# Reordering VectorE, TensorE and GpSimd work where an attention kernel hands over to its first expert

## The chip, the cores and the metric

One Trainium2 chip (trn2), one core. The metric is the device time of one execution in microseconds. Times before are the median of three runs; the profile is one more execution of the same program, taken by the hardware profiler.

## The reference

Eight batches of eight heads of 576 tokens go through masked attention; the result, seen as 4608 rows of 512, is routed to one of eight experts each (top 1), and the expert's two-layer network is scaled by two gates.

```python
scores = np.where(masks, scale * q @ k.T, -1e9)
attn = exp(scores - max) / (sum + 1e-9)
x = (attn @ v).transpose(0, 2, 1, 3).reshape(4608, 512)
logits = x @ w_gate;  e_idx = argmax(logits, axis=1)
gate_w = softmax(logits)[arange, e_idx]
eom = sigmoid(x @ w_output_gate)
for e in range(8):
    mask = e_idx == e
    h = maximum(x[mask] @ w1[e], 0)          # 512 -> 1024
    out[mask] = gate_w * eom[:, e] * (h @ w2[e])   # 1024 -> 512
```

## The kernel before

**Attention and gating.** `attention()` walks 8 batches in 5 steps each. Behind each batch `gating()` computes the choice of expert for 576 tokens, laid out as 96 partitions by 6 columns. It gives each token a slot number among the tokens of its expert, makes one-hot tables of the slots (`hit`: 128 places and 48 pages), and multiplies them with values to be delivered (`named`, line 694). Matmuls on TensorE (`place`, line 593) add these up into `book`, a table of token numbers and gates by place, page and expert. The gate is a 32-bit number, so `parted()` (line 684) cuts it into three bf16 parts: copy, subtract, copy, subtract, copy; each part is one of the last three values of `book`. In the batches up to the second to last this runs beside attention. In the last batch (`last`) nothing of attention is left, and the order of the statements from line 741 on is the order in which each engine sees its work.

**The lead.** After four batches the expert with the most tokens (the lead) is known, and its first 256 rows can start early: `lead_layer()` (line 503) is a generator that issues its first layer in pieces between other work, in single-pass float32. Its eight blocks of 128 hidden columns are taken in four pairs; two pairs' sums live in two PSUM banks (tile `sp`). When a pair is done, `flush()` empties the bank: ScalarE writes the rounded positive part to `hha`, VectorE the difference to `hla`. The fourth pair reuses the second pair's bank, so TensorE must wait for the second pair's `hla`. `fill(n)` advances the generator by n matmuls, each of which is two records in the trace. With `hold[0]` set (from the last batch's second half on), flushes are put off; the list `LF` says how many matmuls are issued at which point of the last gating. The end of it reads, from line 748:

```python
for _ in weights(): pass     # 3 small VectorE operations: the gate
parted()                     # 5 on GpSimd
counts(); count_on()
hold[0] = False
for v in range(2, 2 + WP): name(v)    # 3 on VectorE
fill(LF[1])                  # 11 matmuls, flushes among them
count()
enter(place(2, 2 + WP), 2, 2 + WP)
```

**The experts.** `experts()` (line 1267) first gathers the lead's other rows by indirect DMAs on GpSimd's queue (`gather(0)`, line 158). Weights and activations are split in a high and a low float32r half (`split`, line 994: ScalarE casts, another engine subtracts), and each product is three matmuls: high by high, low by high, high by low. The first 256 rows of the lead go through the second layer as two blocks of 128 rows (`by_token`, `tokens_in`, lines 1109 and 1127), each 8 columns j by 3 matmuls into one PSUM bank. Within the second block the gathered rows are turned (`turn`), and the two last quarters of w1 are split; `TURN_AT` says behind which column. Then come the eight ranks r. For r = 0 the first layer of the lead's other rows runs as 8 columns of 12 matmuls (`layer1`, `products`), rotating over four PSUM banks `hps`. Behind column 3 `copied()` (line 985) makes copies of the page table by 12 matmuls into the bank `hps[3]`, which VectorE copies out; they are read at the second layer of the rank (`by_tail`, line 1156). From there on ranks follow each other, with the next rank's loads, splits and turns within the second layer of the one before.

Of the kernel before, what the change touches and what calls it, by code (L numbers as in the profile page):

```python
# [20 lines left out]
E = 8  # L21
# [5 lines left out]
QB = 96  # L27
# [7 lines left out]
EB = 4  # L35
HALVED = B
STEADY = B - 2
# [5 lines left out]
PN = 4  # L43
LF = (4, 11, 4, 3)
TURN_AT = (1, 3, 4, 6)
# [15 lines left out]
def attn_moe_kernel(  # L61
# [56 lines left out]

    NC = 2 * B - HALVED + 1
    cum = const.tile([QB + 2, NC, E], BF16, name="cum")  # L120
# [52 lines left out]
    def attention():  # L173
        with ExitStack() as actx:
# [234 lines left out]
            def logits(b, hf):  # L409
# [23 lines left out]
                yield 0  # L433
                if b < HALVED and hf == 1:
                    yield from gating(b, 0, NB, b)
                if b >= HALVED:
                    yield from gating(b, JH * hf, JH * (hf + 1), 2 * b - HALVED + hf)

            def count():
                cp = ps_g.tile([128, 512], F32, name="gp")  # L440
                nc.tensor.matmul(out=cp[:, 0:E], lhsT=tri[0:QB, 1, :], rhs=cum[0:QB, 2 * B - HALVED, :], start=True, stop=True)
                nc.vector.tensor_copy(out=cnt, in_=cp[:, 0:E])
# [60 lines left out]
            def lead_layer():  # L503
# [17 lines left out]
                for j in range(0, FC, 2):  # L521
# [14 lines left out]
                    done.append((slice(j, j + 2), hp, []))  # L536
                    if not hold[0]:
                        flush(j + 2)
# [3 lines left out]
            def gating(b, j0, j1, ci):  # L542
# [141 lines left out]
                def parted():  # L684
                    left = wall[:, tcols]
                    for i in range(WP):
                        P.tensor_copy(out=parts[:, i, :], in_=left)
                        if i + 1 < WP:
                            P.tensor_tensor(out=rest[:, i, :], in0=left, in1=parts[:, i, :], op=ALU.subtract)
                            left = rest[:, i, :]  # L690
# [36 lines left out]
                else:  # L727
# [6 lines left out]
                    if not last:  # L734
                        for _ in weights():
                            pass
                        parted()
                        for v in range(2, 2 + WP):
                            name(v)
                    else:  # L740
                        fill(LF[0])
                        wp = place(0, 2)
                        enter(before, 0, 2 + WP)
                        exp_sum()
                        enter(wp, 0, 2)
                        for _ in tokens_first(0, HB, idx0):
                            pass
                        for _ in weights():
                            pass
                        parted()  # L750
                        counts()
                        count_on()
                        hold[0] = False
                        for v in range(2, 2 + WP):
                            name(v)
                        fill(LF[1])
                        count()
                        enter(place(2, 2 + WP), 2, 2 + WP)
                if ci == EB - 1:
# [7 lines left out]
            def fill(n):  # L767
                for _ in range(n):
                    for g in fillers[:1]:
                        if next(g, 1):  # L770
                            fillers.clear()
# [221 lines left out]

    def split(hi, lo, src, eng=nc.vector):
        nc.scalar.copy(out=hi, in_=src)  # L995
        eng.tensor_tensor(out=lo, in0=src, in1=f32(hi), op=ALU.subtract)  # L996

# [42 lines left out]

    def split_w(r, which, c, eng=nc.vector):
        raw = raws[r, which, c]
        if which == 1:
            split(w1h[:, c, :], w1l[:, c, :], raw, eng)
        else:
            sl = slice(2 * c, 2 * c + 2)
            split(w2h[:, sl, :].rearrange("p c f -> p (c f)"), w2l[:, sl, :].rearrange("p c f -> p (c f)"), raw)
# [57 lines left out]
    def trio(i):  # L1105
        hh, hl = hs[i]
        return (hh, w2h), (hl, w2h), (hh, w2l)

    def tokens_in(yp, i, o, m, between={}):
        for j in range(FC):  # L1110
            for q, (h, w) in enumerate(trio(i)):
                nc.tensor.matmul(out=yp[0:m, :], lhsT=h[:, j, o:o + m], rhs=w[:, j, :],  # L1112
                                 start=(j == 0 and q == 0), stop=(j == FC - 1 and q == 2))
            for fn, *a in between.get(j, ()):
                fn(*a)
# [10 lines left out]

    def by_token(i, o, m, w, row, between={}):
        yp = rotate(yps)
        tokens_in(yp, i, o, m, between)
        return lambda: store(yp, w, row, m)  # L1130
# [136 lines left out]
    def experts():  # L1267
# [10 lines left out]
        for c in range(2):  # L1278
            split_w(0, 1, c)
        by_token(0, 0, 128, lead_gate[:, 0:1], tabe[:, 0:1])()  # L1280
        between = {j: [(turn, 0, c, m)] for j, (c, m) in zip(TURN_AT, blocks(0))}
        between[5] = [(arms, 0)]
        for c in range(2, KC):
            between[TURN_AT[c - 2]].append((split_w, 0, 1, c, nc.gpsimd))
        sent = [by_token(0, 128 * c, 128, lead_gate[:, c:c + 1], tabe[:, c:c + 1], between) for c in range(1, EH // 128)]
# [3 lines left out]
        for r in range(E):  # L1289
# [12 lines left out]
            for j in range(FC):  # L1302
                layer1(r, j)
                if r == 0 and j == 1:
                    count_spare()
                    send_away()
                if r == 0 and j == 3:
                    copied()
# [191 lines left out]
```

## Time and profile before

| | |
|---|---|
| median of 3 runs | 624.65 us (624.39 to 625.74) |
| the profiled execution, its own time | 624.76 us |
| span of its trace | 622.5 us |
| mean granted TensorE clock | 0.985 |
| TensorE (PE) busy | 580.3 us, 93% |
| VectorE (DVE) busy | 308.8 us, 50% |
| ScalarE (ACT) busy | 278.1 us, 45% |
| GpSimd (POOL) busy | 202.2 us, 32% |

The span runs from the first to the last instruction; 2.26 us of the execution's time lie outside it. Attention with its gatings takes the first 170 us, the hand-over to the first expert some 30 us, the ranks the rest, with the last matmuls near 609 us. A record of an instruction has its start, its duration, and in brackets the idle time of its engine just before it with what ended that.

### The profile page before, as it was taken

What the parts mean: (1) busy time and instruction counts of PE and PEld (TensorE: products, weight loads), DVE (VectorE), ACT (ScalarE), POOL (GpSimd) and SP (SyncE); (2) the same over time, 40 slices, a digit from 0 to 9 for tenths busy, and PEclk for the clock granted to TensorE, in tenths of its full rate; (3) what the DMA queues carried; (4) which work ended last, traced back from release to release, by engine and by line L of the source; (5) the groups of instructions that cost most, each with busy time, mean ns of one, the idle gap of its engine ahead of it and who ended that gap; (6) DMA issues with size and microseconds to landing.
All of it is one profiled execution on the core that took longest, in us unless ns stands there. A gap on an engine that the chain in (4) does not pass through costs nothing. (4 is left out here: it accounts for less than half of the span.)

```text
span 622.5 us, 14509 instructions
## 1 busy us (share of the span) xinstructions
PE 580.3 (93%) x5670; PEld 490.8 (79%) x5670; DVE 308.8 (50%) x699; ACT 278.1 (45%) x553; POOL 202.2 (32%) x282
## 2 busy tenths in 40 slices
PE   8898999899849999999999999999999999999990
PEld 6676776777538889988998899889988878888880
DVE  4888888987637553443143325334533542442500
ACT  3877877766225243433243224334243443443310
POOL 4327766665324424011401140225023124021030
PEclk9999999999979999999999999999999999999996
DMA  9989999893422846144305430553064164161010
GB/s 319 311 291 293 310 298 296 291 296 121 160 63 74 326 125 189 35 160 140 127 22 169 153 115 5 183 133 115 14 221 141 55 220 140 49 227 43 3 42 17
DMA packets 42488, 97.93 MB, mean 157 GB/s; under 512 B 5458, under 2 KB 16346, under 8 KB 42394
## 3 DMA queue, kind: packets, MB, share of 16 engines
q1 hardware_dynamic: 34122, 73.47, 36.3%
q0 software_dynamic: 6864, 19.74, 9.6%
q10 hardware_dynamic: 1408, 3.38, 1.5%
q8 instruction: 71, 1.16, 0.8%
q14 instruction: 23, 0.19, 0.1%
HBM read 77.74 MB, written 20.58 MB: 158 GB/s over the span
## 5 line engine op out<-in xcount | busy, mean ns | idle before, releaser
L1078 PE MATMUL hp<-xl,w1h 128*128 128x256 f32 (+8 forms) x384 | 126.9, 330 | 0.1
L1078 PE MATMUL hp<-xh,w1h 128*128 128x256 f32 (+8 forms) x384 | 127.0, 331 | 0.0
L1078 PE MATMUL hp<-xh,w1l 128*128 128x256 f32 (+8 forms) x384 | 126.9, 330 | 0.0
L1112 PE MATMUL yp<-w2h,hhb 128*128 128x512 f32 (+1 forms) x208 | 83.2, 400 | 0.0
L1112 PE MATMUL yp<-w2l,hhb 128*128 128x512 f32 (+1 forms) x208 | 81.3, 391 | 0.0
L1112 PE MATMUL yp<-w2h,hlb 128*128 128x512 f32 (+1 forms) x208 | 81.1, 390 | 0.0
L1199 POOL DMA_INDIRECT out_dram<-ys,idx x32 | 32.9, 1029 | 132.7 <-ACT ys L1198 128.2
L1199 POOL DMA_INDIRECT out_dram<-ys,ri x18 | 20.3, 1126 | 169.4 <-ACT ys L1198 166.3
L1078 PEld LDWEIGHTS hp<-xl,w1h 128*128 128x128 f32 x384 | 72.6, 189 | 3.4 <-DVE xl L996 0.4
L1078 PEld LDWEIGHTS hp<-xh,w1h 128*128 128x128 f32 x384 | 72.6, 189 | 3.4 <-ACT xh L995 0.3
L1078 PEld LDWEIGHTS hp<-xh,w1l 128*128 128x128 f32 x384 | 72.6, 189 | 2.8
L996 DVE TENSOR_TENSOR xl<-tp,xh 128x512 fp32r<-128x512 f32 (+3 forms) x40 | 25.8, 650 | 88.1 <-ACT xh L995 84.4
L995 ACT CAST xh<-tp 128x512 fp32r<-128x512 f32 (+3 forms) x40 | 22.0, 555 | 99.2 <-PE tp L1055 96.0
L1101 DVE SCALAR_TENSOR_TENSOR hlb<-hp,hhb 128x384 fp32r<-128x384 f32 (+3 forms) x48 | 28.2, 590 | 68.1 <-ACT hf L1100 64.2
L1098 ACT ACTIVATE hhb<-hp 128x384 fp32r<-128x384 f32 (+3 forms) x48 | 24.9, 518 | 81.8 <-PE hp L1078 73.5
L309 POOL TENSOR_TENSOR p_t<-p_t,st 128x512 f32<-128x512 f32 x40 | 42.6, 1064 | 52.0 <-DVE cum L584 15.2
L158 POOL DMA_INDIRECT xg<-xd,idx x40 | 44.0, 1101 | 23.9 <-DVE f L665 9.9
L1112 PEld LDWEIGHTS yp<-w2l,hhb 128*128 128x128 f32 (+1 forms) x208 | 38.8, 187 | 8.7
L1112 PEld LDWEIGHTS yp<-w2h,hhb 128*128 128x128 f32 (+1 forms) x208 | 38.9, 187 | 8.1 <-issue 0.4
L1198 ACT ACTIVATE ys<-yp,pages 128x512 f32<-128x512 f32 (+1 forms) x36 | 24.9, 692 | 45.0 <-issue 35.5
L1112 PEld LDWEIGHTS yp<-w2h,hlb 128*128 128x128 f32 (+1 forms) x208 | 38.9, 187 | 7.7
L996 DVE TENSOR_TENSOR w1l<-raw,w1h 128x1024 fp32r<-128x1024 f32 x30 | 36.7, 1225 | 11.7 <-ACT w1h L995 11.3
(213 smaller groups left out, 1079.0 us busy)
## 6 DMA issues: line engine op xcount, KB each, us to landing
raw<-in_moe_w_dram SPq DMA_DIRECT2D x54, 512.0 KB
vst<-in_vs_dram SPq DMA_DIRECT2D x8, 780.0 KB
vlt<-in_vl_dram SPq DMA_DIRECT2D x16, 292.5 KB
q_t<-in_ql_dram SPq DMA_DIRECT2D x8, 576.0 KB
q_t<-in_qs_dram SPq DMA_DIRECT2D x7, 650.0 KB
xd<-x_t SPq DMA_DIRECT2D x80, 54.0 KB
xd<-x_t SPq DMA_DIRECT2D x16, 256.0 KB
raw<-in_moe_w_dram ACTq DMA_DIRECT2D x6, 512.0 KB
```

Of the source, the lines that this page charges most:

```text
L158: nc.gpsimd.indirect_dma_start(out=dst, out_offset=None, in_=src, in_offset=bass.IndirectOffsetOnAxis(ap=idx, axis=0), bounds_check=top, o ...
L309: nc.gpsimd.tensor_tensor(out=p_t, in0=p_t, in1=st, op=ALU.subtract)
L995: nc.scalar.copy(out=hi, in_=src)
L996: eng.tensor_tensor(out=lo, in0=src, in1=f32(hi), op=ALU.subtract)
L1078: nc.tensor.matmul(out=hp[:, 0:n], lhsT=w[:, k, 128 * j:128 * (j + 1)], rhs=x[:, k, 0:n], start=first, stop=(k == KC - 1 and w is w1l))
L1098: nc.scalar.activation(out=hh[:, j, 0:s], in_=hp[:, 0:s], func=AF.Relu)
L1101: nc.vector.scalar_tensor_tensor(out=hl[:, j, 0:s], in0=hp[:, 0:s], scalar=0.0, in1=f32(hh[:, j, 0:s]), op0=ALU.max, op1=ALU.subtract)
L1112: nc.tensor.matmul(out=yp[0:m, :], lhsT=h[:, j, o:o + m], rhs=w[:, j, :], start=(j == 0 and q == 0), stop=(j == FC - 1 and q == 2))
L1198: nc.scalar.activation(out=ys[0:m, 0:n], in_=yp[0:m, 0:n], func=AF.Copy, scale=w[0:m, :])
L1199: i = nc.gpsimd.indirect_dma_start(out=out.rearrange("t (k d) -> (t k) d", k=k), out_offset=bass.IndirectOffsetOnAxis(ap=row, axis=0), in_ ...
```

## The change

It does four things. (1) In the last batch's gating, the lead's held flushes are allowed before the gate is computed (`hold[0] = False` and one of the matmuls come forward), the gate's parts are made on VectorE instead of GpSimd, behind the matmuls' flushes, and the count of tokens goes behind the last `place`. The flush of the fourth pair moves to the generator's end. (2) In the lead's first block of the second layer the matmuls with the low half of w2 stand two columns later (`lag=2`). (3) The last two quarters of the lead's w1 get their low half from VectorE instead of GpSimd. (4) The copies of the page table are made behind column 5 instead of 3. A constant (`HALVED`) that had no effect is gone.

```diff
-LF = (4, 11, 4, 3)
+LF = (4, 10, 4, 3)
...
                     done.append((slice(j, j + 2), hp, []))
-                    if not hold[0]:
+                    if not hold[0] and j + 2 < FC:
                         flush(j + 2)
                     yield
                 flush(FC)
...
                 def parted():
                     left = wall[:, tcols]
                     for i in range(WP):
-                        P.tensor_copy(out=parts[:, i, :], in_=left)
+                        W.tensor_copy(out=parts[:, i, :], in_=left)
                         if i + 1 < WP:
-                            P.tensor_tensor(out=rest[:, i, :], in0=left, in1=parts[:, i, :], op=ALU.subtract)
+                            W.tensor_tensor(out=rest[:, i, :], in0=left, in1=parts[:, i, :], op=ALU.subtract)
                             left = rest[:, i, :]
...
                         for _ in tokens_first(0, HB, idx0):
                             pass
+                        hold[0] = False
+                        fill(1)
                         for _ in weights():
                             pass
-                        parted()
                         counts()
                         count_on()
-                        hold[0] = False
+                        fill(LF[1])
+                        parted()
                         for v in range(2, 2 + WP):
                             name(v)
-                        fill(LF[1])
+                        enter(place(2, 2 + WP), 2, 2 + WP)
                         count()
-                        enter(place(2, 2 + WP), 2, 2 + WP)
...
-    def tokens_in(yp, i, o, m, between={}):
+    def tokens_in(yp, i, o, m, between={}, lag=0):
+        todo = [[] for _ in range(FC + lag)]
         for j in range(FC):
-            for q, (h, w) in enumerate(trio(i)):
-                nc.tensor.matmul(out=yp[0:m, :], lhsT=h[:, j, o:o + m], rhs=w[:, j, :],
-                                 start=(j == 0 and q == 0), stop=(j == FC - 1 and q == 2))
-            for fn, *a in between.get(j, ()):
+            for q, hw in enumerate(trio(i)):
+                todo[j + (lag if q == 2 else 0)].append((j, *hw))
+        order = [p for ps in todo for p in ps]
+        for n, (j, h, w) in enumerate(order):
+            nc.tensor.matmul(out=yp[0:m, :], lhsT=h[:, j, o:o + m], rhs=w[:, j, :],
+                             start=(n == 0), stop=(n == len(order) - 1))
+            for fn, *a in between.get(n // 3, ()) if n % 3 == 2 else ():
                 fn(*a)
...
-        by_token(0, 0, 128, lead_gate[:, 0:1], tabe[:, 0:1])()
+        by_token(0, 0, 128, lead_gate[:, 0:1], tabe[:, 0:1], lag=2)()
...
-            between[TURN_AT[c - 2]].append((split_w, 0, 1, c, nc.gpsimd))
+            between[TURN_AT[c - 2]].append((split_w, 0, 1, c))
...
-                if r == 0 and j == 3:
+                if r == 0 and j == 5:
                     copied()
```

`W` is VectorE in the last batch and GpSimd in all others, so only the last batch's parts move.

VectorE, end of the last gating (`idx` holds the row numbers for the gathers, `f` and `wall` the gate, `cum` the running counts). Before:

```order
L455 TENSOR_SCALAR idx_70<-tn 128x6
L663 TENSOR_SCALAR f<-f 96x6
L665 SCALAR_TENSOR_TENSOR f<-f 96x6
L668 RECIPROCAL wall<-f 96x6
L575 TENSOR_REDUCE s_3468<-oh 96x8
L584 TENSOR_TENSOR cum<-cum,s_3468 96x8
L694 TENSOR_TENSOR named<-hit,parts 96x6x48 x3
L513 SCALAR_TENSOR_TENSOR hla<-sp,hha 128x512 x3
L442 COPY cnt<-gp 128x8
L604 TENSOR_TENSOR book<-book,gp 128x144
L996 TENSOR_TENSOR w2l<-hhb,w2h 128x1024 x2
```

With the change, first from `idx` on:

```order
L452 TENSOR_SCALAR idx_70<-tn 128x6
L510 SCALAR_TENSOR_TENSOR hla<-sp,hha 128x512
L660 TENSOR_SCALAR f<-f 96x6
L662 SCALAR_TENSOR_TENSOR f<-f 96x6
L665 RECIPROCAL wall<-f 96x6
L572 TENSOR_REDUCE s_3468<-oh 96x8
```

and then from `cum` to the low half of w2:

```order
L581 TENSOR_TENSOR cum<-cum,s_3468 96x8
L510 SCALAR_TENSOR_TENSOR hla<-sp,hha 128x512
L684 CAST parts<-wall 96x6
L686 TENSOR_TENSOR rest<-wall,parts 96x6
L684 CAST parts<-rest 96x6
L686 TENSOR_TENSOR rest<-rest,parts 96x6
L684 CAST parts<-rest 96x6
L691 TENSOR_TENSOR named<-hit,parts 96x6x48 x3
L601 TENSOR_TENSOR book<-book,gp 128x144
L439 COPY cnt<-gp 128x8
L510 SCALAR_TENSOR_TENSOR hla<-sp,hha 128x512
L994 TENSOR_TENSOR w2l<-hhb,w2h 128x1024 x2
```

The three differences of the lead stood in a row behind the names; now the second pair's stands right behind `idx`, the third's ahead of the five operations on the parts, the fourth's behind `book` and `cnt`. TensorE's order around it keeps its 11 matmuls in a row; only the count's matmul moved behind the six of `place`.

TensorE, first matmuls of the lead's first block in the second layer, before:

```order
L1112 MATMUL yp_3614<-w2h,hha 128x512
L1112 MATMUL yp_3614<-w2h,hla 128x512
L1112 MATMUL yp_3614<-w2l,hha 128x512
L1112 MATMUL yp_3614<-w2h,hha 128x512
L1112 MATMUL yp_3614<-w2h,hla 128x512
```

and with the change:

```order
L1114 MATMUL yp_3614<-w2h,hha 128x512
L1114 MATMUL yp_3614<-w2h,hla 128x512
L1114 MATMUL yp_3614<-w2h,hha 128x512
L1114 MATMUL yp_3614<-w2h,hla 128x512
L1114 MATMUL yp_3614<-w2l,hha 128x512
```

The first matmul with the low half of w2 is the fifth instead of the third.

TensorE, the copies of the page table, before:

```order
L1078 MATMUL hp_3613<-xh_3605,w1l 128x408
L1256 UNCONDITIONAL_BRANCH
L991 MATMUL hp_3613<-pages,ident 64x96 x2
L991 MATMUL hp_3613<-pages,ident 32x96 x4
L1256 COMPARE_AND_BRANCH x2
L1078 MATMUL hp_3610<-xh_3605,w1h 128x480
```

and with the change:

```order
L1076 MATMUL hp_3611<-xh_3605,w1l 128x408
L1258 UNCONDITIONAL_BRANCH
L989 MATMUL hp_3613<-pages,ident 64x96 x2
L989 MATMUL hp_3613<-pages,ident 32x96 x4
L1258 COMPARE_AND_BRANCH x2
L1076 MATMUL hp_3612<-xh_3605,w1h 128x480
```

The bank written by the copies (`hp_3613`, `hps[3]`) was the one that the matmul just ahead had filled; now the matmul ahead fills another one (`hp_3611`).

## Rows read from the trace of the kernel before

**Rows 1.** The page: TensorE's busy time, share, instructions; and its waits from 210 us on.

```profile
PE 580.3 (93%) x5670; PEld 490.8 (79%) x5670; DVE 308.8 (50%) x699; ACT 278.1 (45%) x553; POOL 202.2 (32%) x282
...
PE tp L1055 <- PEq L1172: 0.6, 2, 0.3
```

**Rows 2.** Timeline of TensorE: start, duration, line, operation, [idle before, released by].

```profile
165.59 1.90 PE L528 MATMUL sp<-xe,raw 128*128 128x256 f32 x8
168.40 1.53 PE L528 MATMUL sp<-xe,raw 128*128 128x256 f32 x6
177.35 5.57 PE L528 MATMUL sp<-xe,raw 128*128 128x256 f32 x16 [7.43 <-DVE hla L513]
...
184.71 0.47 PE L1112 MATMUL yp<-w2h,hha 128*128 128x512 f32 x1 [1.39 <-DVE book L604]
...
185.81 0.50 PE L1112 MATMUL yp<-w2l,hha 128*128 128x512 f32 x1 [0.39 <-DVE w2l L996]
...
190.93 0.39 PE L1112 MATMUL yp<-w2h,hha 128*128 128x512 f32 x1
...
192.29 0.60 PE L1055 MATMUL tp<-ident,xg 128*128 128x128 f32 x4
```

**Rows 3.** Timeline of VectorE in the same stretch.

```profile
169.65 0.17 DVE L455 TENSOR_SCALAR idx<-tn 128x6 int32<-128x6 f32 x1
...
170.45 0.16 DVE L584 TENSOR_TENSOR cum<-cum,s 96x8 bf16<-96x8 bf16 x1
171.41 0.46 DVE L694 TENSOR_TENSOR named<-hit,parts 96x288 bf16<-96x288 bf16 x1 [0.79 <-POOL parts L687]
...
176.62 0.68 DVE L513 SCALAR_TENSOR_TENSOR hla<-sp,hha 128x512 fp32r<-128x512 f32 x1
...
184.27 0.30 DVE L604 TENSOR_TENSOR book<-book,gp 128x144 f32<-128x144 f32 x1
184.53 2.36 DVE L996 TENSOR_TENSOR w2l<-hhb,w2h 128x1024 fp32r<-128x1024 f32 x2
```

**Rows 4.** Timeline of GpSimd: the gathers of the lead's rows between the parts.

```profile
170.09 1.08 POOL L158 DMA_INDIRECT xg<-xd,idx  x1 [9.92 <-DVE f L665]
...
171.54 1.21 POOL L158 DMA_INDIRECT xg<-xd,idx  x1 [0.16 <-issue]
```

**Rows 5.** Timeline of ScalarE: the fourth pair's flush and the high half of w2.

```profile
182.96 0.60 ACT L512 ACTIVATE hha<-sp 128x512 fp32r<-128x512 f32 x1 [4.97 <-PE gp L441]
183.46 1.98 ACT L995 CAST w2h<-hhb 128x1024 fp32r<-128x1024 f32 x2
```

**Rows 6.** Stretches: length, busy PE, PEld, DVE, ACT, POOL, granted clock, DMA share, GB/s.

```profile
174.50:181.00 6.50, 3.65 (x9) 2.93 (x10) 2.11 (x4) 0.60 (x1) 1.58 (x3) 0.50 0.23 74
...
183.00:186.00 3.00, 1.22 (x9) 0.63 (x7) 2.41 (x5) 3.00 (x4) 0.00 (x0) 1.00 0.00 0
...
178.00:179.00 1.00, 1.00 (x4) 0.82 (x3) 0.69 (x1) 0.00 (x0) 0.00 (x0) 0.50 0.00 0
...
217.00:218.00 1.00, 1.00 (x7) 1.00 (x6) 0.54 (x1) 0.42 (x2) 0.00 (x0) 1.00 0.15 45
```

**Rows 7.** Timeline of TensorE in the lead's first layer and at its end.

```profile
207.16 0.35 PE L1078 MATMUL hp<-xl,w1h 128*128 128x408 f32 x1
207.35 0.35 PE L1078 MATMUL hp<-xh,w1l 128*128 128x408 f32 x1
209.16 0.69 PE L991 MATMUL hp<-pages,ident 128*64 128x96 f32 x12 [1.47 <-DVE hlb L1101]
209.78 0.45 PE L1078 MATMUL hp<-xh,w1h 128*128 128x408 f32 x1
...
220.74 1.09 PE L1055 MATMUL tp<-ident,xg 128*128 128x128 f32 x8
```

**Rows 8.** VectorE: waits from 186 to 200 us (total, times, longest); the last difference.

```profile
DVE xl L996 <- ACT xh L995: 3.2, 4, 1.1
...
198.12 0.56 DVE L996 TENSOR_TENSOR xl<-tp,xh 128x384 fp32r<-128x384 f32 x1 [0.62 <-ACT xh L995]
```

More of the change, by code (lines that the diff above doesn't have):

```diff
@@ L35 @@
 EB = 4
-HALVED = B
 STEADY = B - 2
@@ L117, in attn_moe_kernel @@
     wts, eidx = (ecst[:, i, :] for i in range(2))
-    NC = 2 * B - HALVED + 1
+    NC = B + 1
     cum = const.tile([QB + 2, NC, E], BF16, name="cum")
@@ L433, in logits @@
                 yield 0
-                if b < HALVED and hf == 1:
+                if hf == 1:
                     yield from gating(b, 0, NB, b)
-                if b >= HALVED:
-                    yield from gating(b, JH * hf, JH * (hf + 1), 2 * b - HALVED + hf)
             def count():
                 cp = ps_g.tile([128, 512], F32, name="gp")
-                nc.tensor.matmul(out=cp[:, 0:E], lhsT=tri[0:QB, 1, :], rhs=cum[0:QB, 2 * B - HALVED, :], start=True, stop=True)
+                nc.tensor.matmul(out=cp[:, 0:E], lhsT=tri[0:QB, 1, :], rhs=cum[0:QB, B, :], start=True, stop=True)
                 nc.vector.tensor_copy(out=cnt, in_=cp[:, 0:E])
@@ L992, in copied, with split @@
         nc.vector.tensor_copy(out=copies.rearrange("p f v e k -> p (f v e k)"), in_=hp[:, 0:2 * n])
-    def split(hi, lo, src, eng=nc.vector):
+    def split(hi, lo, src):
         nc.scalar.copy(out=hi, in_=src)
-        eng.tensor_tensor(out=lo, in0=src, in1=f32(hi), op=ALU.subtract)
+        nc.vector.tensor_tensor(out=lo, in0=src, in1=f32(hi), op=ALU.subtract)
     rows_of = lambda r: caps[r] - (0 if r else EH)
@@ L1039, in gather, with split_w @@
             xgs[r, c] = xg
-    def split_w(r, which, c, eng=nc.vector):
+    def split_w(r, which, c):
         raw = raws[r, which, c]
         if which == 1:
-            split(w1h[:, c, :], w1l[:, c, :], raw, eng)
+            split(w1h[:, c, :], w1l[:, c, :], raw)
         else:
@@ L1125, in strip_in, with by_token @@
                                  start=(j == 0), stop=(j == FC - 1))
-    def by_token(i, o, m, w, row, between={}):
+    def by_token(i, o, m, w, row, between={}, lag=0):
         yp = rotate(yps)
-        tokens_in(yp, i, o, m, between)
+        tokens_in(yp, i, o, m, between, lag)
         return lambda: store(yp, w, row, m)
```

## The prediction

> **What bounds the kernel now.** I read the page first: TensorE is busy for 580.3 us of 622.5 and no other engine comes near [rows 1]. So I asked for TensorE's waits. From 210 us to the end there are two of 0.3 us each [rows 1]; whatever makes TensorE reach 210 us earlier makes the end earlier by as much, as long as weights and rows still arrive in time. The waits that can be removed lie between 168 and 210 us, and the timelines show who ends them.
>
> The largest is 7.43 us, ended by VectorE's `hla` [rows 2]. TensorE finishes the lead's third pair at 168.40 + 1.53 = 169.93 and starts the fourth at 177.35, since it needs the bank that VectorE empties from 176.62 for 0.68 us [rows 3]. That `hla` could have run at 169.8. It stands in VectorE's queue behind three names, and these wait for the gate's parts from GpSimd, whose small operations stand between the gathers, each over 1 us long [rows 4]. The fourth pair then runs slowly: 16 records take 5.57 us, where 8 took 1.90 at 165.59 [rows 2]. The granted clock from 174.5 to 181 is 0.50, the 1.2 GHz level, after TensorE had stood idle since 169.93; from 183 to 186 it is 1.00 again, the 2.4 GHz level, although TensorE is busy for just 1.22 of those 3 us [rows 6].
>
> Two smaller waits follow: 0.39 us for the low half of w2 at 185.81 [rows 2], and 1.47 us at 209.16 for VectorE's difference of column 3, whose bank the page copies want [rows 7].
>
> **The change part by part.**
>
> *The lead's fourth pair starts earlier.* The second pair's `hla` now follows `idx`, which starts at 169.65. VectorE's pace on such small operations is 0.16 us (`cum`, the fifth after `idx`, starts at 170.45 [rows 3]). So `hla` starts at 169.81; plus 0.68 for itself, plus 0.05 for the signal (176.62 + 0.68 = 177.30, TensorE at 177.35 [rows 2, 3]), TensorE starts at 170.54. That is 6.81 us earlier, with 0.61 us of idling left. It can't be more than 7.42, since the third pair ends at 169.93.
>
> *Its clock.* With 0.61 us idle in place of 7.43 I expect the 2.4 GHz level throughout: 183 to 186 shows that gaps of 1.39 and 0.39 us leave it there [rows 2, 6]. 16 records then take two stretches of 1.90, less one drain that is counted twice: a record starts about every 0.22 us, so 3.65 in place of 5.57, a gain of 1.92. The bounds are 0 (clock falls anyway) and 1.92. The fourth pair ends at 174.19 instead of 182.92.
>
> *The parts and names on VectorE.* Behind the first `hla` (170.49) stand five small operations (0.8 us by the same pace), the third pair's `hla` (0.68; ScalarE's `hha` for it waits for the `hla` before, 0.60 us, and is done at 171.1), five operations for the parts (each waits for the one before, so I give them 0.2; 1.0) and three names of at most 0.46 (1.3). That makes 174.3. The `place` that needs the names comes behind the fourth pair, which ends at 174.19, so the parts cost nothing on the path, but there is no cover left: each 0.1 us that they are late is 0.1 us for what follows.
>
> *From the fourth pair to the second layer.* Before, this took 184.71 - 182.92 = 1.79 us: ScalarE's `hha` (0.60) and the first cast of w2 (half of 1.98), with `book` on VectorE ending last at 184.57 [rows 3, 5]. Now the same two on ScalarE go from 174.2 to 175.8. On VectorE `book` (0.30), `cnt` (0.16) and the fourth `hla` (0.68) follow `place` and end near 175.9, and the first matmul needs all three. So TensorE starts at 176.0, a gap of 1.8. I take 0 for this term, with -0.3 to +0.5 as bounds.
>
> *Low w2 two columns later.* The first block took 190.93 - 184.71 = 6.22 us [rows 2]. Six matmuls of the second block take 192.29 - 190.93 = 1.36, so 24 would take 5.44, plus about 0.1 for the first: 0.68 us are lost to the third matmul's wait. Now the first low half is wanted by the fifth matmul, at 176.0 + 4 x 0.23 + 0.1 = 177.0. VectorE starts on it at 175.9, when the fourth `hla` ends and the cast is there, and takes half of 2.36 [rows 3]: 177.05, with the signal 177.1. A wait of 0.1 us and its restart remain, so I take a gain of 0.44, between 0 and 0.68.
>
> *Low w1 on VectorE.* Two subtractions of 1.18 each (the size is that of w2's, 2.36 for two [rows 3]) join the four differences of the turned rows. VectorE idles 3.2 us there, waiting for ScalarE four times [rows 8], and 2.36 fit in. Placed one by one between ScalarE's casts, they put the second and third difference back by 0.3 to 0.7 us, but the last, which the first layer waits for, stays where it was (it starts behind ScalarE, after 0.62 us of idling before). I take 0; the bounds are 0 and the difference 2.36 - 0.62 = 1.74 if they all bunch up ahead of the last one.
>
> *Page copies behind column 5.* Between the last matmul of column 3 and the first of column 4 lie 209.78 - 207.35 = 2.43 us [rows 7]. Without wait and copies a matmul follows after 0.19 (207.16 to 207.35); the copies themselves (209.16 to 209.78, 0.62) are still paid, behind column 5. The gain is 2.43 - 0.19 - 0.62 = 1.62. At column 5 the bank has been free for over 2 us. What may be late next is column 7, which wants the bank back: a column of 12 matmuls takes 2.2 us, and ScalarE, the difference of column 5 and VectorE's copy need about 2.1 of the 2.8 us between. I take 1.62, bounds 1.0 and 1.62.
>
> **The sum.** 6.81 + 1.92 + 0 + 0.44 + 0 + 1.62 = 10.79, taken as 10.8 us. The profiled execution took 624.76 us, 0.11 above the median of 624.65; so 614.0 us.
>
> **Rivals.**
>
> *The clock stays low (6%).* If TensorE's shortened idling still brings the 1.2 GHz level, the fourth pair gives back 1.92 us: 615.9. For it: before, the level fell with less than 5 us of idling [rows 2, 6]. Against: TensorE is now busy for most of 165 to 174.
>
> *VectorE and GpSimd hold each other up (9%).* The gathers run back to back from 170.09 without the parts between, until about 175 (four; the first two take 1.08 and 1.21 [rows 4]), and now VectorE's parts and names run through all of it. If each had to wait for a gather's end, the last name would end at 176 rather than 174.3: 1.7 us, 615.7. What speaks against it: a name that started at 171.41 took 0.46 us although a gather began at 171.54; what suffered, if anything, is the gather, with 1.21 against 1.08 for the one that met no name [rows 3, 4]. The gathers can bear that. The Trainium skill says in "SBUF — State Buffer", section "Who interferes with whom", that a VectorE instruction with two SBUF inputs contends with a GpSimd instruction that reads SBUF, and that whichever starts first holds the shared ports for its whole instruction; by that rule, if a gather counts as such, the time would be this rival's, and the row at 171.41 bears it out at most the other way round.
>
> *Given back at the first expert's end (7%).* With 1.62 us less in the first layer, the turned rows of the next rank come sooner: they are turned at 220.74, and the transfers die down in 217 to 218 (share 0.15 [rows 6, 7]). That leaves 2.7 us, of which 1.62 are taken. If weights or rows are late by more, or column 7 waits for the copies, up to 1.62 are lost: 615.6.
>
> *The flushes don't move as they read (2%).* If TensorE's fourth pair still waits for a later VectorE operation, such as the third pair's `hla` (172.0 instead of 170.5), 1.5 us are lost: 615.5.
>
> *Slower than before (2%).* TensorE turned the first block of gathered rows at 192.29 [rows 2]; now it comes there at about 183.0, 9.2 us sooner by the first four terms. The transfers of the gathers had ended by 178 (DMA share 0.00 from 178 to 179 [rows 6]), so nearly 5 us are left. But VectorE now works almost without a pause from 170 on, and if GpSimd's gathers were held up by that work until it pauses, the rows would come late. From 193.8 on (183.0 + 10.8) the wait would eat the whole gain; at 196.8 the time would be 627.8.
>
> **How the numbers follow.** The forecast has 74%. Its own bounds are 614.0 - 0.61 - 0.24 - 0.3 = 612.85 and, with half of the costs of the terms at their bad ends (0.3, 0.4, 0.5), about 615.2. The rivals at 615.5 to 615.9 are near; two of them together can make 617. The three runs spread by 1.35 us, so I put the range at 612.4 to 616.8. What a measurement can tell from no change is 0.2%, 1.25 us here. All cases but the last are faster by far more: 0.97 for faster, 0.01 for the same, 0.02 for slower.
>
> **What would show it.** Right: TensorE's 7.43 us wait becomes about 0.6 us, the granted clock reads 1.00 from 170 to 183, the fourth pair takes 3.65 us, the second layer starts near 176.0, its fifth matmul waits about 0.1, no wait at the page copies, and all waits from 200 us on as before. Wrong: names or `book` as the releaser of a wait over 1 us at 174 to 177; a clock of 0.50 anywhere from 170 to 185; a gather's transfer as releaser of the first turn; a new wait of TensorE behind 200 us. A time above 617 would mean that a term of the first stage, not one of the small ones, was read wrongly.

## The result, and the profile after

The changed kernel takes 615.29 us (median of four runs, 614.29 to 619.59) where the kernel before took 625.19 beside it (624.39 to 626.30): a ratio of 0.985 [0.980, 0.990]. The forecast was 614.0, with a range from 612.4 to 616.8. The profiled execution took 615.36 us; its trace spans 613.3.

First the page of the changed kernel (TensorE's busy time hardly moved, its share rose, as against [rows 1]) and TensorE's waits from 160 to 215 us and from 200 us on (total, times, longest):

```profile
PE 579.9 (95%) x5670; PEld 490.0 (80%) x5670; DVE 313.4 (51%) x706; ACT 279.0 (45%) x553; POOL 195.4 (32%) x275
...
PE yp L1114 <- ACT w2h L993: 1.2, 1, 1.2
PE gp L594 <- DVE named L691: 0.7, 1, 0.7
PE sp L525 <- DVE hla L510: 0.5, 1, 0.5
...
PE tp L1053 <- PEq L1174: 0.6, 2, 0.3
```

The wait of 7.43 us for `hla` is 0.5, the one at the copies is gone, and from 200 us on nothing new has appeared. The second line, 0.7 us for the first names, was there before too, at 168.13. TensorE's timeline:

```profile
169.60 0.43 PE L594 MATMUL gp<-named,hit 96*128 96x96 bf16 x6 [0.66 <-DVE named L691]
169.86 1.53 PE L525 MATMUL sp<-xe,raw 128*128 128x256 f32 x6
171.93 3.72 PE L525 MATMUL sp<-xe,raw 128*128 128x256 f32 x16 [0.54 <-DVE hla L510]
175.50 0.54 PE L594 MATMUL gp<-named,hit 96*128 96x144 bf16 x6
...
177.27 0.50 PE L1114 MATMUL yp<-w2h,hha 128*128 128x512 f32 x1 [1.22 <-ACT w2h L993]
...
178.07 0.39 PE L1114 MATMUL yp<-w2h,hla 128*128 128x512 f32 x1
178.53 0.50 PE L1114 MATMUL yp<-w2l,hha 128*128 128x512 f32 x1
...
183.19 0.39 PE L1114 MATMUL yp<-w2h,hha 128*128 128x512 f32 x1
...
184.55 0.60 PE L1053 MATMUL tp<-ident,xg 128*128 128x128 f32 x4
...
204.05 0.35 PE L1076 MATMUL hp<-xh,w1l 128*128 128x408 f32 x1
204.33 0.69 PE L989 MATMUL hp<-pages,ident 128*64 128x96 f32 x12
204.95 0.45 PE L1076 MATMUL hp<-xh,w1h 128*128 128x408 f32 x1
```

Against [rows 2, 7]: the 16 records of the fourth pair take 3.72 us instead of 5.57 and follow the third pair's end (171.39) after 0.54 us; the second layer starts 1.62 us behind them instead of 1.79; the first block takes 5.92 us instead of 6.22; the copies have no idle time ahead of them. VectorE, GpSimd and ScalarE in the same stretch, to be held against [rows 3, 4, 5]:

```profile
171.11 0.17 DVE L452 TENSOR_SCALAR idx<-tn 128x6 int32<-128x6 f32 x1
171.19 0.68 DVE L510 SCALAR_TENSOR_TENSOR hla<-sp,hha 128x512 fp32r<-128x512 f32 x1
...
173.20 0.16 DVE L684 CAST parts<-wall 96x6 bf16<-96x6 f32 x1
173.40 0.16 DVE L686 TENSOR_TENSOR rest<-wall,parts 96x6 f32<-96x6 f32 x1
173.59 0.30 DVE L684 CAST parts<-rest 96x6 bf16<-96x6 f32 x1
...
174.20 1.25 DVE L691 TENSOR_TENSOR named<-hit,parts 96x288 bf16<-96x288 bf16 x3
176.07 0.30 DVE L601 TENSOR_TENSOR book<-book,gp 128x144 f32<-128x144 f32 x1 [0.63 <-PE gp L438]
...
176.37 0.68 DVE L510 SCALAR_TENSOR_TENSOR hla<-sp,hha 128x512 fp32r<-128x512 f32 x1
```

```profile
171.55 1.06 POOL L157 DMA_INDIRECT xg<-xd,idx  x1 [9.92 <-DVE idx L452]
172.92 1.00 POOL L157 DMA_INDIRECT xg<-xd,idx  x1 [0.30 <-issue]
```

```profile
176.18 1.99 ACT L993 CAST w2h<-hhb 128x1024 fp32r<-128x1024 f32 x2
```

`hla` stands right behind `idx`, and the names end at 175.45, 0.2 us ahead of the fourth pair. No gather is longer than 1.06 us.

The granted clock of two stretches of the changed kernel (length, busy PE with records, clock, DMA share, GB/s), and of the earlier one in the kernel before:

```profile
24.00:28.00 4.00, 4.00 (x57) 0.57 0.77 250
165.00:186.00 21.00, 18.52 (x101) 1.00 0.29 97
```

```profile
24.00:28.00 4.00, 3.22 (x89) 1.00 0.93 280
```

From 165 to 186 us the clock is at the 2.4 GHz level throughout, as forecast. But `idx` is reached at 171.11 instead of 169.65 [rows 3]: 1.46 us **later**, in a stage that the change does not touch. The profiled execution had the 1.2 GHz level for part of 24 to 28 us, in the midst of attention, and the one before had not. So the comparisons below are counted from the six products of 96x96 of the last gating (168.13 before, 169.60 after) to the end of the span: 454.37 us before, 443.70 after, 10.67 us less; the forecast's terms had a sum of 10.79.

### The profile page after: what moved, and what is told of

Its sections match the earlier page's. It is cut to its first block, busy times and chain, and to the rows that moved or that the text cites. A ratio compares the mean times of both kernels' runs of the same rounds, so it can differ in the third digit from the quotient of the medians.

```text
span 613.3 us, 14510 instructions
## 1 busy us (share of the span) xinstructions
PE 579.9 (95%) x5670; PEld 490.0 (80%) x5670; DVE 313.4 (51%) x706; ACT 279.0 (45%) x553; POOL 195.4 (32%) x275
## 5 line engine op out<-in xcount | busy, mean ns | idle before, releaser
L994 DVE TENSOR_TENSOR w1l<-raw,w1h 128x1024 fp32r<-128x1024 f32 x32 | 39.1, 1225 | 11.9 <-ACT w1h L993 11.8
```

What stands on the lines that cost most here:

```text
L994: nc.vector.tensor_tensor(out=lo, in0=src, in1=f32(hi), op=ALU.subtract)
```

## The experiments

The time of a run moves by several us with attention alone (below), more than most parts of the change are worth. So each part is read from the trace, from the products of 96x96 to the end of the span:

| kernel | products at | from there to the end | median of its runs |
|---|---|---|---|
| before | 168.13 | 454.37 | 625.19 |
| after | 169.60 | 443.70 | 615.29 |
| parts alone | 170.86 | 450.54 | 621.07 |
| order of the differences alone | 168.40 | 450.30 | 621.28 |
| names twice | 167.74 | 446.26 | 615.43 |
| no lag, copies at column 3 | 168.23 | 447.47 | 617.68 |
| low w1 on GpSimd | 167.86 | 443.64 | 613.74 |
| names ahead | 168.84 | 443.66 | 614.95 |
| names ahead, cast cut | 172.03 | 443.37 | 615.54 |
| names ahead, no lag | 167.44 | 445.96 | 615.29 |
| third difference early | 167.71 | 442.69 | 612.82 |
| the change again | 168.66 | 443.74 | 614.73 |

The kernel before, run beside them, had medians of 627.74 us (with the first four experiments of the table), 625.37 (the next four) and 626.17 (the last two).

**Is the later attention part of the change?**

> The changed kernel once more, unaltered, on the same chip as its variant. If attention's length is spread between executions, its `idx` stands anywhere from 169 to 174 us and the time moves with it, while from `idx` to the end of the span there are 442.2 us as in the first profile, with a granted clock of 1.00 from 165 to 186 us and waits of 0.54, 1.22 and 0.23 us at the same places. If the 1.46 us by which the first profile was later belonged to the program, `idx` stands at 171.1 again.

The unaltered kernel reached `idx` at 170.17 and took 442.23 us from there (442.19 the first time), with the same waits and this clock:

```profile
165.00:186.00 21.00, 18.52 (x103) 1.00 0.26 88
```

Over all twelve profiles the products stand anywhere between 167.44 and 172.03 us, and kernels of both orders lie at both ends of it: the parts alone, an edit of the kernel before, at 170.86, the names computed twice, an edit of the changed one, at 167.74. So attention's 1.46 us do not belong to the change. In the latest of all (names ahead, cast cut), the clock had fallen twice:

```profile
24.00:28.00 4.00, 4.00 (x72) 0.57 0.89 263
136.00:141.00 5.00, 4.30 (x57) 0.66 0.70 233
```

At a mean clock of 0.57, 4 us do the work of 2.3, so one such fall can cost 1.7 us (an estimate), about the 1.46 seen. It isn't all: the parts alone came 2.7 us late without a clock below 1.00 before 168 us. Nor is a fall always paid: with low w1 on GpSimd the clock was 0.51 from 8 to 11 us, and its products, at 167.86, are among the earliest. What else spreads attention wasn't tried.

**The parts on VectorE alone** (kernel before, two lines of `parted()`).

```diff
-                        P.tensor_copy(out=parts[:, i, :], in_=left)
+                        W.tensor_copy(out=parts[:, i, :], in_=left)
...
-                            P.tensor_tensor(out=rest[:, i, :], in0=left, in1=parts[:, i, :], op=ALU.subtract)
+                            W.tensor_tensor(out=rest[:, i, :], in0=left, in1=parts[:, i, :], op=ALU.subtract)
```

> The kernel before, with one part of the change alone: the last batch's gate parts on VectorE instead of GpSimd; the order of the lead's differences is left as it was, behind the names. Times are counted from the start of the `idx` row on VectorE. My theory (the fourth pair waits for whatever stands ahead of its `hla` on VectorE): parts and names now run without GpSimd, so `hla` comes 3.2 us behind `idx` and the fourth pair starts at idx + 3.9 instead of idx + 7.70, after 3.7 us of idling. Its clock is open: 3.7 us for its 16 records if the granted clock stays at 1.00, 5.6 us if it falls to 0.50 as after 7.43 us. The time falls by 3.8 us (clock 0.50) to 5.7 us (clock 1.00). Rival (VectorE and GpSimd hold each other up while the four gathers run): names and parts take visibly longer than the 0.16 to 0.20 and 0.42 us of the changed kernel and the fourth pair starts at idx + 5 or later. On attention, where the profiled changed kernel reached `idx` 1.46 us later: if that is spread between executions, `idx` stands anywhere around 169 to 171.5 us; if it is the program, it stands at 169.65 within 0.3, as in the kernel before.

TensorE's fourth pair, and the clock as above:

```profile
176.34 5.41 PE L528 MATMUL sp<-xe,raw 128*128 128x256 f32 x16 [3.69 <-DVE hla L513]
```

```profile
176.00:180.00 4.00, 3.66 (x9) 0.57 0.60 176
```

The pair starts at idx + 3.96 and 3.83 us are won, as forecast for a low clock. Half of the idling already costs nearly the whole slow pair: 3.69 us of it left 5.41 us for 16 records, where 7.43 had left 5.57 [rows 2].

**The order of the differences alone** (kernel before; parts stay on GpSimd).

```diff
-LF = (4, 11, 4, 3)
+LF = (4, 10, 4, 3)
...
-                    if not hold[0]:
+                    if not hold[0] and j + 2 < FC:
                         flush(j + 2)
...
+                        hold[0] = False
+                        fill(1)
                         for _ in weights():
                             pass
                         parted()
                         counts()
                         count_on()
-                        hold[0] = False
+                        fill(LF[1])
                         for v in range(2, 2 + WP):
                             name(v)
-                        fill(LF[1])
-                        count()
                         enter(place(2, 2 + WP), 2, 2 + WP)
+                        count()
```

> The kernel before, with the other part alone: the lead's differences put ahead of the names, and the parts left on GpSimd between its gathers; no lag of low w2, low w1 on GpSimd, page copies behind column 3 as before. My theory: the fourth pair starts at idx + 0.8, takes 3.7 us at a granted clock of 1.00 and ends at idx + 4.5, as in the changed kernel. The parts are done at idx + 6.6 as in the kernel before, the last name at idx + 7.0, its product is added to `book` at idx + 7.6 to 7.9, and the fourth `hla` stands behind that, to idx + 8.7. If the first matmul of the second layer needs that `hla`, as my sum assumed, it starts at idx + 8.75; if it needs only the cast of w2 and TensorE's own order, at idx + 7.8 to 8.0. (Kernel before: idx + 15.06; changed kernel: idx + 6.16.) The time falls by 6 to 6.4 us against the kernel before, so the move of the parts alone is worth another 2 us or so on top. Rival (the differences' place is all, the parts' engine is worth nothing): second layer at idx + 6.2, the time 8.9 us below the kernel before. `idx` itself: 169.65 within 0.3 if attention's 1.46 us belong to the program, anywhere if they are spread.

```profile
170.73 3.72 PE L528 MATMUL sp<-xe,raw 128*128 128x256 f32 x16 [0.54 <-DVE hla L513]
177.24 0.88 PE L597 MATMUL gp<-named,hit 96*128 96x144 bf16 x6 [2.80 <-DVE named L694]
...
178.69 0.76 PE L1113 MATMUL yp<-w2h,hha 128*128 128x512 f32 x1 [0.56 <-DVE cnt L442]
```

```profile
177.00:184.00 7.00, 5.75 (x18) 0.51 0.04 12
```

The fourth pair does what it does in the changed kernel. But the names, late on GpSimd, now hold up the product behind it for 2.80 us, and the clock falls after that and stays low until 184 us. So 4.07 us are won, not the 6 or more that I expected: I had not priced the clock. Each half alone wins some 4 us (3.83 and 4.07), since each leaves a wait of about 3 us that brings the 1.2 GHz level.

The second layer's start at idx + 8.78 is the figure expected if it waits for the fourth `hla`. The rows speak against that reading: that `hla` ran from 178.46 for 0.68 us, so it was still running when the matmul started at 178.69, which `cnt` had released. A time that fits is not a releaser.

**Is there cover for the names?** (Changed kernel.)

```diff
-                        for v in range(2, 2 + WP):
+                        for v in (*range(2, 2 + WP), *range(2, 2 + WP)):
                             name(v)
```

> The changed kernel with the three last names computed twice on VectorE (1.25 us more work ahead of the product that needs them). My theory (no cover is left): names end at idx + 5.6 instead of idx + 4.34, the fourth pair still ends at idx + 4.54, `book` and the fourth `hla` come 1.2 us later, and the time rises by 1.1 us. Within that: if the first matmul of the second layer needs the fourth `hla`, it starts at idx + 7.3; if it is the cast of w2 on ScalarE that it waits for, it starts at idx + 6.2 to 6.4 as before and the fifth matmul, which needs the low half of w2 from VectorE, waits 1.1 us instead. Rival (the cast alone bounds this place, VectorE has slack): the time rises by less than 0.3 us.

```profile
174.75 0.54 PE L594 MATMUL gp<-named,hit 96*128 96x144 bf16 x6 [0.96 <-DVE named L691]
...
175.62 0.68 DVE L510 SCALAR_TENSOR_TENSOR hla<-sp,hha 128x512 fp32r<-128x512 f32 x1
175.85 0.47 PE L1114 MATMUL yp<-w2h,hha 128*128 128x512 f32 x1 [0.56 <-DVE cnt L439]
...
177.49 0.79 PE L1114 MATMUL yp<-w2l,hha 128*128 128x512 f32 x1 [0.47 <-DVE w2l L994]
```

```profile
177.00:181.00 4.00, 3.52 (x10) 0.57 0.01 2
```

No cover is left: the product waits 0.96 us for the names, and 2.56 us are lost (446.26 against 443.70), where I expected 1.1. Some 1.7 of them are the clock, which falls in the first block: 4.00 x (1 - 0.57). The second layer starts at idx + 6.60, later than with the cast as the only bound (6.16) and while the fourth `hla` (175.62 for 0.68) still runs. `cnt` released it, and it does not need that `hla`.

**The lag and the copies undone** (changed kernel).

```diff
-        by_token(0, 0, 128, lead_gate[:, 0:1], tabe[:, 0:1], lag=2)()
+        by_token(0, 0, 128, lead_gate[:, 0:1], tabe[:, 0:1])()
...
-                if r == 0 and j == 5:
+                if r == 0 and j == 3:
                     copied()
```

> The changed kernel with two of its small parts undone, which lie 20 us apart and are read each in its own stretch: low w2 in step with the high half again in the lead's first block, and the page copies behind column 3 again. My theory: the third matmul of the first block waits for the low half until 1.25 us behind the first, so the block takes 6.25 us instead of 5.92 (+0.33); the copies wait again for VectorE's difference of column 3, and between the last matmul of column 3 and the first of column 4 lie 2.4 us instead of 0.19, of which 0.6 were paid behind column 5 (+1.5 to 1.6). In all +1.9 us against the changed kernel. Rival for the lag (the second layer is bound by casts and differences that come one by one, so later matmuls wait instead): block 5.9 us either way. Rival for the copies (column 7 pays in the changed kernel what column 4 saves): less than 1 us between the two kernels from the first column to the strips. `idx` at 171.11 within 0.3 if attention's 1.46 us belong to the program, anywhere around 169 to 171.5 if they are spread.

```profile
175.90 0.50 PE L1114 MATMUL yp<-w2h,hha 128*128 128x512 f32 x1 [1.23 <-ACT w2h L993]
...
177.16 0.50 PE L1114 MATMUL yp<-w2l,hha 128*128 128x512 f32 x1 [0.53 <-DVE w2l L994]
...
185.29 0.60 PE L1053 MATMUL tp<-ident,xg 128*128 128x128 f32 x4
...
202.29 0.69 PE L989 MATMUL hp<-pages,ident 128*64 128x96 f32 x12 [1.59 <-DVE hlb L1099]
```

```profile
178.00:182.00 4.00, 4.00 (x12) 0.57 0.00 0
```

Twice the expected 1.9 us: 3.77. The copies cost 1.65 of it (from the first layer's first matmul to the strips behind its last, 20.83 us against 19.18). The other 2.12 come from the lag. Of these only 0.4 are the third matmul's wait; after it the clock falls for most of 178 to 182 us, which costs 1.7. From the second layer's first matmul to the first turn it takes 9.39 us instead of 7.28. So **with the lag undone, what the fourth pair won by its fast clock is given back 7 us later**.

**The lag once more, with the names ahead.**

> The kernel with the names ahead, and low w2 in step with the high half again (no lag). It asks what made the granted clock fall to 0.50 at 178.4 us in the kernel with neither lag nor late copies: there TensorE stood idle for 0.54, 1.23 and 0.53 us within 8 us (2.3 in all), in the changed kernel for 0.54, 1.22 and 0.23 (2.0 in all) with the clock at 1.00. Here I expect 0.05, 1.2 and 0.5 us (1.8 in all). If the idling of that stretch as a whole decides, the clock stays at 1.00, and the block takes 6.25 us; if the third matmul's wait of 0.5 us decides by itself, the clock falls in this block again and costs about 1.9 us more.

```profile
175.09 0.50 PE L1114 MATMUL yp<-w2h,hha 128*128 128x512 f32 x1 [2.02 <-ACT w2h L993]
...
176.35 0.80 PE L1114 MATMUL yp<-w2l,hha 128*128 128x512 f32 x1 [0.53 <-DVE w2l L994]
```

```profile
176.00:180.00 4.00, 3.65 (x9) 0.57 0.10 38
```

With the lag, the kernel with the names ahead has this clock:

```profile
165.00:186.00 21.00, 18.26 (x104) 1.00 0.30 99
```

Without it the clock falls again and 2.30 us are lost (445.96 to 443.66), 2.01 of them between the second layer's first matmul and the first turn. The run does not settle what I asked: the wait for the cast was 2.02 us and not 1.2, so the idling was longer, not shorter, than in the kernel it was to be compared with. One figure in the question was also of another kind: the 0.23 us of the changed kernel count from start to start, beyond the usual step. As idle time, like the other waits, it is 0.07 us (178.07 + 0.39 to 178.53). What stands: in the two kernels without lag, one profile each, the level fell; in the six profiles with lag and the names once it was 1.00 from 165 to 186 us. The times of the pair with the names ahead don't show the loss (medians of 615.29 and 614.95 us, four runs each). Whether the clock falls in every execution without lag is not shown.

**Low w1 on GpSimd again** (changed kernel; `split` and `split_w` take the engine as an argument again).

```diff
-            between[TURN_AT[c - 2]].append((split_w, 0, 1, c))
+            between[TURN_AT[c - 2]].append((split_w, 0, 1, c, nc.gpsimd))
```

> The changed kernel with its second two subtractions for low w1 on GpSimd again, as before the change. My theory (the term was worth 0): the second block and the turns take 7.21 us to the first layer's first column either way, and the time is that of the changed kernel within 0.1 us from `idx` on. Rival (the two subtractions of 1.2 us bunch up ahead of the last difference of the turned rows): the changed kernel pays up to 1.74 us for them, and this one shows a shorter stretch. As nothing ahead of that place differs from the changed kernel, it also repeats its first stretch: fourth pair at idx + 0.82 for 3.72 us, second layer at idx + 6.16, a granted clock of 1.00 throughout, if that clock follows from the order alone; a fall to 0.50 somewhere in 174 to 181 us if it hangs on chance with waits of 0.54, 1.22 and 0.23 us. `idx` itself: anywhere from 169 to 172.5 us, as in the five profiles so far.

From `idx` to the first layer's first matmul it takes 19.31 us with GpSimd and 19.29 with VectorE; from the products to the end 443.64 and 443.70. The part is worth nothing, as forecast. GpSimd needs 4.75 us for the two subtractions, VectorE 1.23 for each, and both are covered.

**VectorE's order, changed further.** The second pair's `hla` goes ahead of `idx`, the names ahead of the counts.

```diff
+                        hold[0] = False
+                        fill(1)
                         for _ in tokens_first(0, HB, idx0):
                             pass
-                        hold[0] = False
-                        fill(1)
                         for _ in weights():
                             pass
-                        counts()
-                        count_on()
-                        fill(LF[1])
                         parted()
                         for v in range(2, 2 + WP):
                             name(v)
+                        counts()
+                        count_on()
+                        fill(LF[1])
                         enter(place(2, 2 + WP), 2, 2 + WP)
```

> The changed kernel with VectorE's order changed once more: the second pair's `hla` ahead of the four small operations that make `idx`, and the parts and names ahead of the counts and of the third pair's `hla`. Counted from the third pair's end. My theory (what stands ahead on VectorE is what the fourth pair and the second layer wait for, and the fourth `hla` is not waited for by the first matmul): the fourth pair starts 0.05 us after the third one's end instead of 0.54, with the granted clock at 1.00; the names end 0.7 us sooner, ahead of the fourth pair's end; the second layer still waits for ScalarE's cast of w2, 1.6 us behind the fourth pair's end; so 0.5 us less from `idx` on, about 0.6 counted from the end of attention's last `book`. Rival (a later `idx` makes the gathers late): gathers come 0.7 us later, and TensorE waits for the first turned rows. Rival (the fourth `hla`, now right behind the third, bounds the second layer): gap 1.9 us or more behind the fourth pair.

The next run adds:

```diff
-        for c in range(4):
+        raw = raws[0, 2, 0]
+        for a in range(2):
+            split(w2h[:, a, :], w2l[:, a, :], raw[:, 512 * a:512 * (a + 1)])
+        for c in range(1, 4):
             split_w(0, 2, c)
```

> The kernel with the names ahead, and ScalarE's first cast of w2 (and VectorE's subtraction for it) cut into its two columns. If ScalarE's `hha` and cast are what the second layer's first matmul waits for, it starts 1.15 us behind the fourth pair's end instead of 1.6, and the fifth matmul, which wants the low half of the first column, waits about 0.2 us: 0.3 us less than with the cast whole. If it is `book` or `cnt` on VectorE (0.56 us behind them was the wait with the names computed twice), the start is 1.0 to 1.2 us behind too, and a cut finer than this would bring nothing. If it is the fourth `hla`, nothing changes: 1.6 us.

With the whole cast, the third and fourth pair run as one (22 records in a row), but nothing is won (443.66, where I expected 0.5 us less). TensorE and ScalarE in that kernel:

```profile
169.11 4.98 PE L525 MATMUL sp<-xe,raw 128*128 128x256 f32 x22
...
176.49 0.50 PE L1114 MATMUL yp<-w2h,hha 128*128 128x512 f32 x1 [2.02 <-ACT w2h L993]
```

```profile
174.91 0.60 ACT L509 ACTIVATE hha<-sp 128x512 fp32r<-128x512 f32 x1 [3.64 <-DVE hla L510]
```

The gap behind the fourth pair grew from 1.62 to 2.40 us: the fourth `hha` waited for the third pair's `hla`, which I had put behind the names (174.14 for 0.68). The rows show that order only; that the two share the tile `hha` is from the code. With the cast cut in two (one column each) the gap is 1.97 and 0.3 us are won, as expected in size, though with the same wait. So the last version puts that `hla` back to its place and keeps the cut:

```diff
                         for _ in weights():
                             pass
+                        fill(LF[1])
                         parted()
...
                         counts()
                         count_on()
-                        fill(LF[1])
```

> The kernel with the names ahead and the first cast of w2 cut in two, and the third pair's `hla` put back between the weights and the parts. In the two runs with the names ahead the fourth `hha` on ScalarE did not wait for the fourth pair but for that third `hla`, and the second layer began 2.40 us (whole cast) and 1.97 us (cut cast) behind the fourth pair, against 1.62 in the changed kernel, which ate the 0.5 us won at its start. My theory: with the third `hla` done early, `hha` follows the fourth pair at once, the names end 0.35 us behind the fourth pair, and the first matmul waits for `cnt` or for the half cast, 1.3 us behind the fourth pair; counted from the start of the last gating product but one (96x96) on TensorE to the end of the span, about 442.8 us, against 443.7 for the changed kernel and 443.4 for the kernel with the cut cast. Rival (the place is bound by something else on VectorE, such as the fourth `hla`): gap 1.6 us or more, 443.1 or more. As a time that is 0.15%, less than the spread of the runs.

```profile
167.97 4.98 PE L525 MATMUL sp<-xe,raw 128*128 128x256 f32 x22
...
174.22 0.47 PE L1114 MATMUL yp<-w2h,hha 128*128 128x512 f32 x1 [0.56 <-ACT w2h L993]
```

The gap is 1.27 us and 442.69 us remain, 1.0 less than with the change. Its runs have a median of 612.82 us (612.57 to 614.78), the change beside it 614.73 (613.56 to 615.66); ratios to the kernel before 0.979 [0.976, 0.982] and 0.981 [0.978, 0.985]. The trace shows the 1.0 us; in the time, the intervals overlap.

## Why the prediction was right, step by step

The sum was right within 0.12 us (10.79 against 10.67, from the products on), and most of its terms one by one (the rows of one profile on either side):

| step | forecast | measured, after against before |
|---|---|---|
| fourth pair earlier | 6.81 (0.61 idle left) | 6.88 (0.54 left) |
| its clock | 1.92 | 1.85 |
| to the second layer | 0 (-0.3 to 0.5) | 0.17 won |
| low w2 two columns later | 0.44 | 0.30 |
| low w1 on VectorE | 0 | 0 |
| page copies behind column 5 | 1.62 | 1.53 |

The measured time stands 1.3 us above the forecast (615.29 against 614.0). In the profiled execution (615.36) that is attention: it was 1.46 us late at `idx`. The sum was made as if that stage always took the same; twelve profiles spread by 4.6 us there. My range took in only the three runs' 1.35 us. Its upper end was also added up too low: half of the terms' bad ends is 0.25 + 0.22 + 0.87 + 0.31 = 1.65 us and not 1.2.

Three steps were reasoned wrongly or too narrowly although their numbers held.

*From the fourth pair to the second layer.* I wrote that the first matmul needs ScalarE's cast, `book` and the fourth `hla`. It does not need the last: four kernels start while it runs (order of the differences alone, names twice, cast cut, third difference early). It was released by the cast, which ends at about 177.2 in the changed kernel; the sum came out since the cast and `hla` end within 0.15 us of each other there. In the changed kernel it is therefore the cast that had to end sooner; halving it was tried with the names ahead alone, where it won 0.3 us.

*The clock and the lag were priced as if apart.* The 1.9 us of the clock were credited to the fourth pair, and 0.44 to the lag. In the two profiles with the new order and no lag, the level falls in the first block instead, and 2.1 and 2.0 us are lost by the first turn. So in these profiles the lag is what keeps the 1.9 us; taken out of the finished kernel it is worth five times its term. The lag was in the change for another reason, so that the sum held here was luck. The rival "the clock stays low" was tied to the fourth pair alone, at 6%; the same mechanism one block later was not on the list.

*No cover left.* That was right, and the price too small: I wrote that 0.1 us of lateness costs 0.1. With 1.25 us more work, 2.56 us were lost, as the clock fell behind the wait.

Of the rivals, the mutual holding up of VectorE and GpSimd fell: names end 4.34 us behind `idx`, forecast 4.65, and the gathers are no longer than before. Nothing was given back at the first expert's end: from the strips behind column 7 to the last matmul (218.85 to 607.37 before, 209.58 to 598.10 after) both traces need 388.5 us. The gathered rows were not late: the first turn's row shows no wait.

## What to carry to other kernels

When two engines feed one place, moving only one of them turns one wait into another: here each half won 4 us, and both with the lag 9. Price a wait of TensorE with the clock it can cost behind it, also one of half a microsecond that stands close to others, and ask for the granted clock of the next 10 us, not only of the stretch that the change was made for. And when a stage that nobody touched moves by more than the terms, count from a common instruction behind it.

## What the runs showed of the hardware

*Small waits can bring the clock down.* It fell to the 1.2 GHz level behind waits of 0.54, 1.23 and 0.53 us, with TensorE at work between them, and did not behind 0.54, 1.22 and 0.07 us. With the names ahead it fell behind 2.02 and 0.53 us and did not behind 2.02 and 0.06. The lag alone does not prevent it: with the names computed twice it fell behind 0.54, 0.96, 0.56 and 0.47 us. It did not behind 1.39 and 0.39 us in the kernel before [rows 2, 6]. A mean of 0.57 over 4 us in the hand-over cost about 1.7 us; in attention that price is an estimate. Which combination decides stays open. The Trainium skill's page "TensorE: Matmul & The Clock Gate", section "Part 1: The HAM clock gate (the "warmup" mystery)", says that the hardware gates the clock to one of two levels by how busy TensorE has lately been; the rows here agree, with 0.50 and 1.00, and show in addition that half a microsecond more of waiting can go with a fall.

*A cast on VectorE that meets a gather's end is held up to it.* In the changed kernel one cast of a part takes 0.30 us and the others 0.16 or 0.17. It ends at 173.89, 0.03 us ahead of the end of the gather that began at 172.92. The cast of the same size at 173.20 and the subtraction at 173.40 lay within the same gather and took their normal 0.16. In all nine other profiles with the parts on VectorE there is such a cast too, of 0.29 to 0.39 us, and each ends 0.02 to 0.03 us ahead of a gather's end. The Trainium skill's page "SBUF — State Buffer", section "Who interferes with whom", says that casts can be among the VectorE instructions that share ports with GpSimd, and that the later one blocks for the other's whole instruction. Here a gather of 1.00 us held one cast for 0.14 us and an earlier one not at all, so the rows do not show a hold for the whole gather; that the ports are the reason no run shows.
